# Logits of an attention unit: from three tiled visits on four PSUM banks to two visits on six

## The chip, the cores and the metric

The kernel runs on one core of a Trainium2 chip. The metric is the time of one execution on the device, in microseconds (us). All executions told of here are fast, with a granted TensorE clock of 0.997 to 1.000. Engines are called PE (TensorE), PEld (its weight loads), DVE (VectorE), ACT (ScalarE), POOL (GpSimd) and SP (which issues DMAs). "Start to start" is the time between the recorded starts of two matmuls in the trace; I use it rather than durations, because matmuls are pipelined (a full one is recorded 380 ns long, and the next starts after 216) and their recorded ends are modelled.

## The reference, cut to what matters

A layer norm of x (2048 tokens x 1024), then the sum of x, an attention branch and a token-mixing MLP. The attention has 32 heads of 32 channels and 4 segments of 512 tokens:

```python
for s in range(N):                                   # 4 segments
    logits = jnp.einsum('bhqd,bhkd->bhqk', qs, ks) * scale + mask   # causal, 512 x 512
    p = _softmax(logits, axis=-1)
    a_dot = jnp.einsum('bhqk,bhkd->bhqd', p, vs)
    pq = phi(qs)
    ...                                              # memory read: a_mem = pq M / (pq z)
    o = g * a_mem + (1.0 - g) * a_dot
    pk = phi(ks)
    M = M + jnp.einsum('bhld,bhle->bhde', pk, vs)    # memory update
    ...
return o @ wo
```

## The kernel before

Four heads of one segment are a *unit*; there are 32. For each unit PE computes logits (transposed: keys on the partitions), ACT takes Exp out of PSUM, POOL sets the masked triangle of the diagonal blocks to zero, and PE weighs the values with the result. Keys come in four blocks of 128. For key block kb only the queries from 128 kb on count, so a head needs 512, 384, 256 and 128 columns for blocks 0 to 3: 1280 float32 columns. The kernel divides PSUM, the memory that PE writes to, into eight banks of 512 such columns.

A head has 32 channels, so its logits matmul fills only 32 of the 128 rows of PE's array. The kernel puts the four heads of a unit on the four 32-row tiles, each writing to its own bank, and they stream side by side (four starts within 10 ns in the trace). I call one such stay in the tiled mode a *visit*. Between visits PE runs full-array matmuls that it has anyway, of the MLP and of the output projection (`main_emit(n)` emits n of them, each 512 columns).

```python
PT_OFF = [0, 512, 896, 1152]
...
    LOGIT_STEPS = [[0], [1], [2, 3]]

    def logits(self, u, step):
        ...
        with fw.group(reads=[self.R_kT[k], self.R_qT[k]], writes=self.R_bank[0:4]):
            col = 0
            for kb in kbs:
                n_q = SEG_L - P * kb
                for r in range(4):
                    fw.mm(self.ps[:, r, col:col + n_q], self.kT[k][32 * r:32 * r + 32, kb * P:(kb + 1) * P],
                          self.qT[k][32 * r:32 * r + 32, kb * P:SEG_L],
                          start=True, stop=True, tile_position=(32 * r, 0))
                col += n_q
        ...
        fw.op("act", lambda e: e.activation(self.pT[:, :, off:off + total], self.ps[:, 0:4, 0:total],
                                            ACT.Exp, scale=SCALE), ...)
        ...                                  # POOL: affine_select on each diagonal block
```

The loop over units (cut); `weigh` of query block qb uses bank 4 + qb % 2, the projections of the unit after next use banks 0, 1 and 2, the full matmuls accumulate in banks 6 and 7:

```python
            self.logits(u, 0)
            self.main_emit(n0)
            ...
            self.logits(u, 1)
            self.main_emit(n1)
            self.logits(u, 2)
            ...
            self.main_emit(n2)
            self.weigh(u, 0)
            self.weigh(u, 1)
            self.proj_q(un, 0)          # ACT evacuates; Exp of q from the second segment on
            self.weigh(u, 2)
            self.proj_v(m, u % 4, 2)
            self.weigh(u, 3)
            self.proj_k(un, 1)          # DVE evacuates, then ACT takes Exp ("etmp") of the same bank
            self.main_emit(n3)
...
            return (10, 8, 7, 7) if u < N_GRP else (10, 8, 8, 8)     # n0..n3; the last units differ
```

The softmax here doesn't subtract the row's maximum and nothing guards it: scores larger than these inputs give would overflow.

Of the kernel before, what the change touches and what calls it, by code (L numbers as in the profile page):

```python
# [6 lines left out]
ACT = mybir.ActivationFunctionType  # L7
# [9 lines left out]
SEG_L = 512  # L17
F_MLP = 3584
P = 128
# [3 lines left out]
SCALE = float(D_HEAD) ** -0.5  # L23
# [5 lines left out]
N_GRP = N_HEAD // 4  # L29
N_UNIT = N_SEG * N_GRP  # L30
VW = D_HEAD + 1
GW = 4 * VW
PT_OFF = [0, 512, 896, 1152]
PT_COLS = 1280


# [279 lines left out]
def _after(*groups):  # L316

    toks = {}
    for r in groups:
        for t in list(r.r.values()) + ([r.w] if r.w is not None else []):  # L320
            cur = toks.get(t.key)
            if cur is None or cur.val < t.val:
                toks[t.key] = t
    return toks
# [21 lines left out]
class _Kernel:  # L346
# [428 lines left out]
        self.fw.dma(self.pk[j][:], self.mtmp[1][:], reads=[self.R_mtmp[1]], writes=[self.R_pk[j]], transpose=True)  # L775


    LOGIT_STEPS = [[0], [1], [2, 3]]

    def logits(self, u, step):  # L780
        fw = self.fw
        k = u % 3
        kbs = self.LOGIT_STEPS[step]
        total = sum(SEG_L - P * kb for kb in kbs)
        with fw.group(reads=[self.R_kT[k], self.R_qT[k]], writes=self.R_bank[0:4]):
            col = 0
            for kb in kbs:
                n_q = SEG_L - P * kb
                for r in range(4):
                    fw.mm(self.ps[:, r, col:col + n_q], self.kT[k][32 * r:32 * r + 32, kb * P:(kb + 1) * P],  # L790
                          self.qT[k][32 * r:32 * r + 32, kb * P:SEG_L],
                          start=True, stop=True, tile_position=(32 * r, 0))
                col += n_q
        off = PT_OFF[kbs[0]]
        fw.op("act", lambda e: e.activation(self.pT[:, :, off:off + total], self.ps[:, 0:4, 0:total],  # L795
                                            ACT.Exp, scale=SCALE),
              reads=self.R_bank[0:4],
              writes=[self.R_pTu[kb] for kb in kbs] + [self.R_pTd[kb] for kb in kbs])
        for kb in kbs:
            d = self.pT[:, :, PT_OFF[kb]:PT_OFF[kb] + P]  # L800
            fw.op("pool", lambda e: e.affine_select(d, d, pattern=[[0, 4], [1, P]], compare_op=ALU.is_ge,  # L801
                                                    fill=0.0, base=0, channel_multiplier=-1),
                  reads=[self.R_pTu[kb]], writes=[self.R_pTd[kb]])

    def weigh(self, u, qb):
# [14 lines left out]
        with fw.group(reads=reads, writes=[self.R_bank[b]]):  # L820
            for r in range(4):
                for kb in range(qb + 1):
                    col = PT_OFF[kb] + (qb - kb) * P
                    fw.mm(self.ps[:, b, VW * r:VW * r + VW], self.pT[:, r, col:col + P], vA[:, kb, hl + r, :],
# [121 lines left out]
    def attention_and_out(self):  # L946
        fw = self.fw
        self.main_init()
        fw.dma(self.wo_sb[:], self.A_wo.rearrange("(jc p) j -> p jc j", p=P), writes=[self.R_wo])
        self.stg_ring.ensure(0)  # L950
        self.proj_q(0, 4)
        self.proj_k(0, 5)
        self.k_transpose(0)
        self.gates()
        for c in range(4):
            self.proj_v(0, c, c)
        self.proj_q(1, 4)
        self.proj_k(1, 5)
        self.main_emit(8)

        def last_of_seg(u):
            return u % N_GRP == N_GRP - 1

        for u in range(N_UNIT):
            s = u // N_GRP
            un, m = u + self.LEAD, u // 4 + 1
            n0, n1, n2, n3 = self.share(u)
            if u == N_GRP:
                wait = _after(*[self.R_xnT[c] for c in range(4)])
                self.oT[1] = self.xnT[0]  # L970
                self.R_oT[1] = [Res(f"oT1_{g}", wait) for g in range(N_GRP)]
            self.logits(u, 0)
            if u and last_of_seg(u - 1):
                self.o_transpose_dma(u - 1)
            self.main_emit(n0)
            if u and not last_of_seg(u - 1):
                self.combine(u - 1)
            self.logits(u, 1)
            self.main_emit(n1)
            self.logits(u, 2)  # L980
            if u + 1 < N_UNIT and (u + 1) // N_GRP < N_SEG - 1:
                self.k_transpose(u + 1)
            if u and not last_of_seg(u - 1):
                self.o_transpose_dma(u - 1)
            self.main_emit(n2)
            self.weigh(u, 0)
            self.weigh(u, 1)
            if un < N_UNIT:
                self.proj_q(un, 0)
            else:  # L990
                self.main_emit(8)
            self.weigh(u, 2)
            if m < 2 * N_SEG:
                self.proj_v(m, u % 4, 2)
            self.weigh(u, 3)
            if un < N_UNIT:
                self.proj_k(un, 1)
            if last_of_seg(u):
                self.combine(u)
            self.main_emit(n3)  # L1000
        assert self.main_k == len(self.main)
        self.tail()

    @staticmethod
    def share(u):

        if u < N_UNIT - 4:
            return (10, 8, 7, 7) if u < N_GRP else (10, 8, 8, 8)
        return (10, 9, 8, 10) if u < N_UNIT - 2 else (10, 9, 8, 4)

    def tail(self):
        fw = self.fw
# [59 lines left out]
```

## Time and profile before

| | before |
|---|---|
| time, median of the first 3 runs | 704.21 us (703.87 to 705.7) |
| span of the profiled execution | 702.2 us |
| one unit, first logits matmul to the next unit's | 14.65 us in the first segment, 15.19 us in most later ones |

From the page of the kernel before: the busy time of each engine with its share of the span, and the chain of work that ended last, by engine.

```profile
PE 688.9 (98%) x4724; PEld 322.7 (46%) x4814; DVE 258.5 (37%) x578; ACT 277.5 (40%) x301; POOL 100.8 (14%) x156
...
PE 95%; DMA 1%; issue 1%; DVE 1%; SPq 0%; ACT 0%; ACTq 0%
```

PE is the bound, and the chain is PE almost from end to end. The list of PE's waits in the kernel before (who waited for whom, us in total, times, longest) says that it hardly ever waits:

```profile
PE ps_all L194 <- DVE h L661: 1.9, 1, 1.9
PE ps_all L194 <- issue: 1.6, 10, 0.2
PE ps_all L194 <- DVE brow_51 L518: 1.3, 1, 1.3
PE ps_all L194 <- DVE stg_1573 L939: 0.7, 1, 0.7
PE ps_all L200 <- DVE o_s_1564 L877: 0.2, 1, 0.2
```

So a change pays only if it shortens what PE itself does between one matmul and the next. The timeline of PE in the kernel before, around the three visits of unit 13 (start and length in us, then the instructions; L194 is the line of the helper that issues every matmul; `32*128` is a 32-row tile, x4 are four matmuls, and the shape shown is that of the first):

```profile
409.81 0.38 PE L194 MATMUL ps_all<-wo_sb,oT_1569 128*128 128x512 bf16 x1
410.12 0.40 PE L194 MATMUL ps_all<-qT_1550,kT_1553 32*128 32x512 bf16 x4
410.44 0.39 PE L194 MATMUL ps_all<-wo_sb,oT_1569 128*128 128x512 bf16 x1
...
412.40 0.38 PE L194 MATMUL ps_all<-gT,w2h_895 128*128 128x512 bf16 x1
412.71 0.34 PE L194 MATMUL ps_all<-qT_1550,kT_1553 32*128 32x384 bf16 x4
412.98 0.39 PE L194 MATMUL ps_all<-gT,w2h_895 128*128 128x512 bf16 x1
...
414.50 0.38 PE L194 MATMUL ps_all<-gT,w2h_895 128*128 128x512 bf16 x1
414.81 0.34 PE L194 MATMUL ps_all<-qT_1550,kT_1553 32*128 32x256 bf16 x8
415.09 0.39 PE L194 MATMUL ps_all<-gT,w2h_895 128*128 128x512 bf16 x1
```

Read the starts, not the lengths. Full matmuls follow one another every 216 ns. In front of a visit it is 0.31 us from the last full matmul to the first logits matmul (312 ns is the median of all visits), 96 ns more than a full matmul needs. Behind the visit it is 0.32, 0.27 and 0.15 us from the last logits matmul to the next full one (medians 317, 264 and 147 ns, after 512, 384 and 128 columns). At 512 columns in 216 ns, 384 take about 162 and 128 about 54 (estimates), so 93 to 102 ns of each are not streaming. A visit therefore costs about 200 ns of PE time on top of its columns. It is the tiled mode, not the smallness of the matmuls: the weighing matmuls have 33 columns each, run on the full array, and start 25 ns apart, and the next projection's first matmul starts 26 ns after the last of them. The Trainium skill, "TensorEngine Tiling (Array Packing)", section Key Properties, states that changing the tiling mode drains the TensorE; these gaps are in line with that.

One more reading. In units 1 to 8 the first visit starts late. From the timeline of the kernel before, at unit 3:

```profile
259.23 0.81 PE L194 MATMUL ps_all<-gT,w2h_896 128*128 128x512 bf16 x3
259.35 0.60 ACT L758 ACTIVATE etmp_1566<-ps_all 128x512 bf16<-128x512 f32 x1 [2.55 <-DVE kT_1553 L755]
...
260.09 0.40 PE L194 MATMUL ps_all<-qT_1549,kT_1552 32*128 32x512 bf16 x4
```

The Exp of the next keys (`etmp`, out of bank 1) ends at 259.95, and the first logits matmul, which writes bank 1, starts 0.14 us after that. In these units it is 432 ns from the last full matmul to the first logits matmul in place of 312.

### The profile page before, as it was taken

Reading aid. Unit: us, or ns where it says so; the run is one execution under the profiler, and the core shown is the slowest. Engines: PE = TensorE matmul, PEld = TensorE weight load, DVE = VectorE, ACT = ScalarE, POOL = GpSimd, SP = SyncE. Lnnn points to the kernel's source line nnn. Section 1 sums busy time; section 2 is a strip of 40 time slices with the busy share of each in tenths; the row PEclk is TensorE's granted clock in tenths of the full one; section 3 lists DMA queues with packets and bytes.
Section 4 is the critical chain, followed back from the end, with each engine's and each line's share of the span. In section 5 each row is a group of like instructions: output and inputs, shape, how many; then the busy total and the mean of one; then the engine's idle time right before and its main releaser. Section 6 shows DMA issues by size and latency. Waiting matters only on the chain.

```text
span 702.2 us, 11155 instructions
## 1 busy us (share of the span) xinstructions
PE 688.9 (98%) x4724; PEld 322.7 (46%) x4814; DVE 258.5 (37%) x578; ACT 277.5 (40%) x301; POOL 100.8 (14%) x156
## 2 busy tenths in 40 slices
PE   8999999999999999999999999999999999999998
PEld 3444444444444444444444444444444444444443
DVE  7730000000012333343454454545546553434444
ACT  7522111111134445444544444444444444443440
POOL 3600000000001111211121211112211111211120
DMA  9497694226044537556264543526173444537003
GB/s 323 98 225 176 139 234 125 61 60 139 1 159 92 114 60 145 120 94 118 50 133 98 112 100 75 128 46 143 34 170 88 86 95 78 114 69 120 23 16 135
DMA packets 210393, 77.17 MB, mean 110 GB/s; under 512 B 172840, under 2 KB 202792, under 8 KB 210344
## 3 DMA queue, kind: packets, MB, share of 16 engines
q1 hardware_dynamic: 209928, 76.06, 47.8%
q8 instruction: 38, 0.62, 0.4%
q10 hardware_dynamic: 416, 0.39, 0.2%
q14 instruction: 11, 0.09, 0.0%
HBM read 59.79 MB, written 5.24 MB: 93 GB/s over the span
## 4 chain that ended last, share of the span: by engine, by line
PE 95%; DMA 1%; issue 1%; DVE 1%; SPq 0%; ACT 0%; ACTq 0%
PE ps_all L194 95%; DMA xin<-in_A_x_dram 1%; SPq L216 0%; DVE prod L873 0%; DVE stg_1573 L939 0%; DVE stg_1571 L939 0%; DVE kT_1552 L755 0%; DVE fin_7784 L1031 0%; DVE ost_1562 L835 0%; ACT etmp_1566 L758 0%; DVE h L661 0%; DVE o_s_1564 L877 0%; PE ps_all L200 0%; DVE srec L871 0%; DVE mtmp_1568 L726 0%
## 5 line engine op out<-in xcount | busy, mean ns | idle before, releaser
L795 ACT ACTIVATE pT<-ps_all 128x1536 bf16<-128x1536 f32 (+1 forms) x96 | 152.9, 1593 | 93.9 <-PE ps_all L194 93.9
L801 POOL TENSOR_SCALAR_AFFINE_SELECT pT<-pT 128x512 bf16<-128x512 bf16 x128 | 84.6, 673 | 564.6 <-ACT pT L795 564.6
L717 ACT ACTIVATE gT<-ps_all,b1c 128x512 bf16<-128x512 f32 x56 | 37.7, 690 | 139.1 <-PE ps_all L194 133.6
L755 DVE CAST kT_1552<-ps_all 128x512 bf16<-128x512 f32 x11 | 7.6, 691 | 170.4 <-PE ps_all L194 170.4
L194 PE MATMUL ps_all<-h,w1s_80 128*128 128x512 bf16 x251 | 55.6, 379 | 0.3
L194 PE MATMUL ps_all<-h,w1s_81 128*128 128x512 bf16 x251 | 55.6, 379 | 0.3
L194 PE MATMUL ps_all<-h,w1s_79 128*128 128x512 bf16 x250 | 55.4, 379 | 0.3
L194 PE MATMUL ps_all<-gT,w2h_895 128*128 128x512 bf16 x219 | 55.1, 380 | 0.4 <-issue 0.2
L194 PE MATMUL ps_all<-gT,w2h_893 128*128 128x512 bf16 x220 | 53.9, 380 | 1.0 <-DVE stg_1573 L939 0.7
L194 PE MATMUL ps_all<-gT,w2h_894 128*128 128x512 bf16 x215 | 53.8, 380 | 0.9 <-issue 0.6
L194 PE MATMUL ps_all<-gT,w2h_896 128*128 128x512 bf16 x217 | 53.9, 380 | 0.6 <-issue 0.3
L835 DVE CAST ost_1561<-ps_all 128x264 bf16<-128x264 f32 (+1 forms) x64 | 23.8, 394 | 64.4 <-PE ps_all L194 64.2
L194 PEld LDWEIGHTS ps_all<-h,w1s_80 128*128 128x128 bf16 x256 | 25.0, 98 | 30.2
L194 PEld LDWEIGHTS ps_all<-h,w1s_79 128*128 128x128 bf16 x256 | 25.0, 98 | 30.2
L194 PEld LDWEIGHTS ps_all<-h,w1s_81 128*128 128x128 bf16 x256 | 25.0, 98 | 30.2
L758 ACT ACTIVATE etmp_1566<-ps_all 128x512 bf16<-128x512 f32 x24 | 14.3, 597 | 58.8 <-DVE kT_1554 L755 20.7
L835 DVE CAST ost_1562<-ps_all 128x264 bf16<-128x264 f32 (+1 forms) x64 | 23.7, 394 | 37.2 <-PE ps_all L194 37.0
L194 PEld LDWEIGHTS ps_all<-gT,w2h_893 128*128 128x128 bf16 x224 | 20.4, 98 | 26.6 <-issue 4.6
L194 PEld LDWEIGHTS ps_all<-gT,w2h_896 128*128 128x128 bf16 x224 | 20.4, 98 | 25.3 <-issue 3.5
L194 PEld LDWEIGHTS ps_all<-gT,w2h_894 128*128 128x128 bf16 x224 | 20.1, 98 | 25.2 <-issue 4.0
L194 PEld LDWEIGHTS ps_all<-gT,w2h_895 128*128 128x128 bf16 x224 | 20.0, 98 | 25.2 <-issue 4.5
L194 PE MATMUL ps_all<-wo_sb,oT_1569 128*128 128x512 bf16 x124 | 30.4, 380 | 0.3 <-issue 0.2
(154 smaller groups left out, 838.6 us busy)
## 6 DMA issues: line engine op xcount, KB each, us to landing
w1s_81<-in_B_w_dram SPq DMA_DIRECT2D x4, 1024.0 KB, 5.7
w1s_79<-in_B_w_dram SPq DMA_DIRECT2D x4, 1024.0 KB, 5.8
w1s_80<-in_B_w_dram SPq DMA_DIRECT2D x4, 1024.0 KB, 5.7
wq_889<-in_A_wq_dram SPq DMA_DIRECT2D x16, 256.0 KB, 4.5
wq_890<-in_A_wq_dram SPq DMA_DIRECT2D x16, 256.0 KB, 3.5
wk_891<-in_A_wk_dram SPq DMA_DIRECT2D x16, 256.0 KB, 4.8
wk_892<-in_A_wk_dram SPq DMA_DIRECT2D x16, 256.0 KB, 3.8
w2h_893<-in_B_w_dram SPq DMA_DIRECT2D x8, 448.0 KB, 4.8
```

The costliest lines, as they stand in the source:

```text
L194: ins = self.nc.tensor.matmul(*args, **kwargs)
L717: fw.op("act", lambda e: e.activation(self.gT[:, fc, half * 512:(half + 1) * 512], self.bank(b), ACT.Gelu_apprx_tanh, bias=self.b1c[:, fc: ...
L755: fw.op("dve", lambda e: e.tensor_copy(self.kT[k][:], self.bank(b)), reads=[self.R_bank[b]], writes=[self.R_kT[k]])
L758: fw.op("act", lambda e: e.activation(self.etmp[1][:], self.bank(b), ACT.Exp), reads=[self.R_bank[b]], writes=[self.R_etmp[1]])
L795: fw.op("act", lambda e: e.activation(self.pT[:, :, off:off + total], self.ps[:, 0:4, 0:total], ACT.Exp, scale=SCALE), reads=self.R_bank[0:4],
L801: fw.op("pool", lambda e: e.affine_select(d, d, pattern=[[0, 4], [1, P]], compare_op=ALU.is_ge, fill=0.0, base=0, channel_multiplier=-1), ...
L835: fw.op("dve", lambda e: e.tensor_copy(dst, self.ps[:, b, 0:n * VW]), reads=[self.R_bank[b]], writes=[self.R_ost[o][qb]])
```

## The change

The intent: two visits a unit in place of three. Blocks 0 and 2 (512 + 256 columns a head) make the first visit. The 1024 columns of block 2 go to banks 4 and 5, two heads to a bank. Blocks 1 and 3 (384 + 128 = 512) make the second, on banks 0 to 3. Two row tiles may not write one bank at the same time (the Trainium skill, "TensorEngine Tiling (Array Packing)", section Restrictions and Gotchas), so in the first visit block 2 of heads 0 and 2 comes first (group 1), then block 0 of all heads (group 2), then block 2 of heads 1 and 3 (group 3), and PE waits before group 3 until its own semaphore tells that group 1 is done. Exp still has three instructions (block 0, block 2, blocks 1 and 3), and the number of full matmuls in a unit stays.

```diff
-PT_OFF = [0, 512, 896, 1152]
+PT_OFF = [0, 768, 512, 1152]
...
-    LOGIT_STEPS = [[0], [1], [2, 3]]
+    LOGIT_STEPS = [[[(0, 2), (2, 2)], [(1, 0), (3, 0), (0, 0), (2, 0)], [(1, 2), (3, 2)]],
+                   [[(0, 1), (1, 1), (2, 1), (3, 1), (0, 3), (1, 3), (2, 3), (3, 3)]]]
...
+        for group in self.LOGIT_STEPS[step]:
+            if len(toks) == 2:
+                fw.E["pe"].eng.wait_ge(toks[0].sem, toks[0].val)
+            banks = self.R_bank[4:6] if group[0][1] == 2 else self.R_bank[0:4]
+            with fw.group(reads=[self.R_kT[k], self.R_qT[k]], writes=banks) as grp:
+                for r, kb in group:
+                    n_q = SEG_L - P * kb
+                    b, col = (4 + r // 2, 256 * (r % 2)) if kb == 2 else (r, 384 if kb == 3 else 0)
+                    fw.mm(self.ps[:, b, col:col + n_q], ...)
+            toks.append(grp.tok)
+        heads = self.ps[:, 0:4, :]
+        if step == 0:
+            self.weights((0,), heads, self.R_bank[0:4])
+            self.weights((2,), self.ps[:, 4:6, :].rearrange("p b (h q) -> p (b h) q", q=256), self.R_bank[4:6])
+        else:
+            self.weights((1, 3), heads, self.R_bank[0:4])
...                                    # weights(): Exp and the masks, as before
-            self.main_emit(n1)
-            self.logits(u, 2)
...
-            return (10, 8, 7, 7) if u < N_GRP else (10, 8, 8, 8)
-        return (10, 9, 8, 10) if u < N_UNIT - 2 else (10, 9, 8, 4)
+            return (11, 14, 7) if u < N_GRP else (11, 15, 8)
+        return (11, 16, 10) if u < N_UNIT - 2 else (11, 16, 4)
```

More of the change, by code (lines that the diff above doesn't have):

```diff
@@ L782, in logits, with weights @@
         k = u % 3
-        kbs = self.LOGIT_STEPS[step]
-        total = sum(SEG_L - P * kb for kb in kbs)
-        with fw.group(reads=[self.R_kT[k], self.R_qT[k]], writes=self.R_bank[0:4]):
-            col = 0
-            for kb in kbs:
-                n_q = SEG_L - P * kb
-                for r in range(4):
-                    fw.mm(self.ps[:, r, col:col + n_q], self.kT[k][32 * r:32 * r + 32, kb * P:(kb + 1) * P],
+        toks = []
+        for group in self.LOGIT_STEPS[step]:
[6 more added lines that the diff above has]
+                    b, col = (4 + r // 2, 256 * (r % 2)) if kb == 2 else (r, 384 if kb == 3 else 0)
+                    fw.mm(self.ps[:, b, col:col + n_q], self.kT[k][32 * r:32 * r + 32, kb * P:(kb + 1) * P],
                           self.qT[k][32 * r:32 * r + 32, kb * P:SEG_L],
                           start=True, stop=True, tile_position=(32 * r, 0))
-                col += n_q
-        off = PT_OFF[kbs[0]]
-        fw.op("act", lambda e: e.activation(self.pT[:, :, off:off + total], self.ps[:, 0:4, 0:total],
-                                            ACT.Exp, scale=SCALE),
-              reads=self.R_bank[0:4],
-              writes=[self.R_pTu[kb] for kb in kbs] + [self.R_pTd[kb] for kb in kbs])
+            toks.append(grp.tok)
[5 more added lines that the diff above has]
+            self.weights((1, 3), heads, self.R_bank[0:4])
+    def weights(self, kbs, src, R_src):
+        fw = self.fw
+        off, total = PT_OFF[kbs[0]], sum(SEG_L - P * kb for kb in kbs)
+        fw.op("act", lambda e: e.activation(self.pT[:, :, off:off + total], src, ACT.Exp, scale=SCALE),
+              reads=R_src, writes=[self.R_pTu[kb] for kb in kbs] + [self.R_pTd[kb] for kb in kbs])
         for kb in kbs:
@@ L966, in attention_and_out @@
             un, m = u + self.LEAD, u // 4 + 1
-            n0, n1, n2, n3 = self.share(u)
+            n0, n1, n2 = self.share(u)
             if u == N_GRP:
@@ L984, in attention_and_out @@
                 self.o_transpose_dma(u - 1)
-            self.main_emit(n2)
+            self.main_emit(n1)
             self.weigh(u, 0)
@@ L999, in attention_and_out @@
                 self.combine(u)
-            self.main_emit(n3)
+            self.main_emit(n2)
         assert self.main_k == len(self.main)
```

## The prediction

> **What bounds the kernel.** TensorE. The profile's first part has PE busy 688.9 of 702.2 us (98%), ACT 40%, DVE 37%, POOL 14%; the chain that ended last is 95% PE; the list of waits gives PE under 6 us of waiting in the whole span. So only PE's own issue time counts; ACT and POOL count only if late.
>
> **Cost of a logits visit now.** Full-array matmuls of 512 columns start every 216 ns (timeline). Start-to-start times around each logits visit (four 32-row tiles side by side), 32 units: last full matmul to first logits matmul 312 ns (96 more than 216); last logits matmul to next full matmul 317 ns after 512 columns, 264 after 384, 147 after 128, each the streaming plus about 100. So a visit pays about 200 ns for entering and leaving the tiled mode. The Trainium skill ("TensorEngine Tiling (Array Packing)", section Key Properties) says that changing the tiling mode drains TensorE; the trace agrees, at about 200 ns a pair. Whole visits, less one 216: step 0 423 ns, step 1 369, step 2 372: 1164 ns a unit. In units 1 to 7 step 0 also waits 120 ns for the Exp of the next keys, 145 ns before its first matmul.
>
> **What the change does.** Matmuls, masks and full matmuls stay; Exp elements too (2048 + 1024 + 2048 in place of 2048 + 1536 + 1536; durations 1.88 and 1.45 us give about 1.02 for 1024, so the sum stays 4.78). It removes one visit a unit: 200 ns x 32 = 6.4 us, all on PE's critical path. Part is given back: in the new step 0 rows 1 and 3 may not write banks 4 and 5 until rows 0 and 2 are done, so the third group waits for PE's own semaphore (same page, Gotcha 1: row tiles may not use one bank at once; no trace here shows a collision). The first 256-column pair is recorded 278 ns long, and its semaphore moves about 28 ns after the recorded end; [...] the third group starts 340 to 400 ns after the first matmul, where the rows are free at about 220. The next full matmul follows 210 ns later.
>
> New step 0: 311 + about 370 + 210 - 216 = 675 (650 to 710). New step 1: 372 + 53 for the longer columns = 425. Together 1100 in place of 1164: 64 ns x 32 = 2.0 us. The 120 ns waits of units 1 to 7 hide behind the first group (banks 4, 5): 0.8 us more.
>
> **New lateness?** Exp of blocks 1 and 3 should end 5.4 us after the unit's first logits matmul, the mask of block 1 at 6.1 (6.4 where DVE slows POOL, seen as 0.93 in place of 0.63 us); the weighing that needs it starts at 6.5 (first segment) to 6.8. Slack 0.3 to 0.7 us: no stall.
>
> **Prediction:** 701.6 us, 8 in 10 between 699.6 and 704.0. Faster by over 2%: 0.01; within 2%: 0.98; slower: 0.01.
>
> **What would show it.** Right: two visits a unit; step 0 near 675 ns, step 1 near 425; PE waits still few; ACT busy unchanged; unit period 60 to 190 ns shorter (now 14.65 and 15.19 us). Wrong: third group at 220 ns (saving 5 us or more), or over 450 (none).
>
> **What would make it wrong.** Release from the own semaphore slower than taken, or row tiles of unlike lengths not streaming side by side; POOL's mask late, so that weighing stalls; a chip that differs by more than these 3 us.

## The result, and the profile after

| | before | changed |
|---|---|---|
| time, median of 4 runs each | 704.77 us (703.87 to 705.7) | 700.17 us (699.74 to 701.33) |
| ratio | | 0.9937, 95% interval 0.9918 to 0.9957 |
| span of the profiled execution | 702.2 us | 698.3 us |
| one unit, first segment / most later ones | 14.65 / 15.19 us | 14.43 / 15.09 us |

A ratio is the mean time of one kernel's fast runs over that of the other's in the same rounds, so it is not quite the ratio of the medians quoted. The kernel became 0.6% faster, which is clear of the noise. It is inside the predicted range and beyond its middle: 4.6 us by the medians and 3.9 by the spans, where the prediction's terms gave 2.8.

From the page of the changed kernel, the same two lines: PE still bounds it, and ACT's busy time is 1.3% less with the same elements: the Exp of block 2 starts 0.1 us before that of block 0 is recorded as ended, so the two overlap in the records.

```profile
PE 686.6 (98%) x4724; PEld 326.1 (47%) x4814; DVE 258.8 (37%) x578; ACT 273.9 (39%) x301; POOL 102.5 (15%) x156
...
PE 96%; DMA 1%; DVE 1%; issue 1%; SPq 1%; ACT 0%; ACTq 0%
```

PE's waits in the changed kernel (the first three of five): still few. The wait on its own semaphore is not among them, because matmuls of groups 1 and 2 are still recorded as running while it lasts.

```profile
PE ps_all L194 <- DVE h L661: 1.8, 1, 1.8
PE ps_all L194 <- DVE brow_51 L518: 1.3, 1, 1.3
PE ps_all L194 <- DVE stg_1573 L952: 0.5, 1, 0.5
```

The timeline of PE in the changed kernel around the two visits of unit 13:

```profile
407.66 0.38 PE L194 MATMUL ps_all<-wo_sb,oT_1569 128*128 128x512 bf16 x1
407.98 0.63 PE L194 MATMUL ps_all<-qT_1550,kT_1553 32*128 32x256 bf16 x8
408.54 0.39 PE L194 MATMUL ps_all<-wo_sb,oT_1569 128*128 128x512 bf16 x1
...
410.70 0.38 PE L194 MATMUL ps_all<-gT,w2h_895 128*128 128x512 bf16 x1
411.02 0.40 PE L194 MATMUL ps_all<-qT_1550,kT_1553 32*128 32x384 bf16 x8
411.35 0.39 PE L194 MATMUL ps_all<-gT,w2h_895 128*128 128x512 bf16 x1
```

And the weight loads of the first of these visits (PEld), which show the groups. Loads of groups 1 and 2 go out together; those of group 3 come 0.35 us after the first, released by PE itself:

```profile
407.97 0.11 PEld L194 LDWEIGHTS ps_all<-qT_1550,kT_1553 32*128 32x128 bf16 x6 [0.42 <-issue]
408.32 0.10 PEld L194 LDWEIGHTS ps_all<-qT_1550,kT_1553 32*128 32x128 bf16 x2 [0.23 <-PE ps_all L194]
408.53 0.11 PEld L194 LDWEIGHTS ps_all<-wo_sb,oT_1569 128*128 128x128 bf16 x2
```

The stretch from the first logits matmul of unit 0 to the start of the last weighing matmul holds all that the change touches. Busy time by engine in that stretch, the kernel before:

```profile
core 0: us, PE busy (x) PEld busy (x) DVE busy (x) ACT busy (x) POOL busy (x), PEclk, DMA share, GB/s
216.16:684.53 468.37, 462.48 (x3697) 220.25 (x3767) 213.56 (x469) 212.47 (x200) 84.62 (x128) 1.00 0.45 92
```

and the changed kernel:

```profile
core 0: us, PE busy (x) PEld busy (x) DVE busy (x) ACT busy (x) POOL busy (x), PEclk, DMA share, GB/s
216.33:680.64 464.31, 459.93 (x3698) 223.71 (x3767) 213.97 (x469) 208.94 (x200) 86.08 (x128) 1.00 0.45 93
```

The stretch is 468.4 before and 464.3 us after: 4.07 us shorter by the exact starts. It is my measure for all experiments, because it repeats: a second profile of the changed kernel has 464.28. What lies ahead of it does not. In the twelve traces, whose opening is the same code, the first logits matmul starts at 216.0 to 218.6 us. From the last weighing matmul to the end it is 17.66 to 17.68 us in all twelve, and the two traces of the changed kernel differ by 1.4 us both in span and in opening. So here the opening makes the spread. Executions of the kernel before over all rounds lie between 703.80 and 707.85 us; the slowest of them have no trace, so what made them slow is not shown.

Where the 4.07 us came from, by starts in the trace. The cost of a visit is from the last full matmul before it to the first full matmul behind it, less one 216; medians of 32 units:

| part | before | changed | difference |
|---|---|---|---|
| visits of a unit | 423 + 369 + 372 = 1164 ns | 657 + 426 = 1083 ns | 81 ns x 32 = 2.6 us |
| first full matmul behind a visit: 226 ns to the next in place of 216 | 3 x 10 ns | 2 x 10 ns | 10 ns x 32 = 0.3 us |
| first visit waits for the Exp of the next keys | 120 ns in 8 units | hidden | 1.0 us |
| one late evacuation, unit 11 (start to start) | 1068 ns | 831 ns | 0.2 us |
| a new wait in unit 8 (below) | none | 0.1 us | -0.1 us |
| sum | | | 4.0 us |

The new wait: in unit 8 of the changed kernel the first output projection (`wo_sb`) starts at 336.36 us, 0.14 us after the DMA transpose of its input has landed (336.23), and 332 ns after the matmul before it in place of 216. Unit 8 takes 15.21 us, against 15.19 before and 15.09 in the units after it.

### The profile page after: what moved, and what is told of

Same layout as the page of the kernel before. It is cut to its first block, busy times and chain, and to the rows that moved or that the text cites. A ratio compares the mean times of both kernels' runs of the same rounds, so it can differ in the third digit from the quotient of the medians.

```text
span 698.3 us, 11157 instructions
## 1 busy us (share of the span) xinstructions
PE 686.6 (98%) x4724; PEld 326.1 (47%) x4814; DVE 258.8 (37%) x578; ACT 273.9 (39%) x301; POOL 102.5 (15%) x156
## 4 chain that ended last, share of the span: by engine, by line
PE 96%; DMA 1%; DVE 1%; issue 1%; SPq 1%; ACT 0%; ACTq 0%
PE ps_all L194 95%; DMA xin<-in_A_x_dram 1%; SPq L216 1%; DVE prod L886 0%; DVE stg_1573 L952 0%; DVE stg_1571 L952 0%; DVE kT_1552 L755 0%; DVE fin_7820 L1042 0%; DVE ost_1562 L848 0%; ACT etmp_1566 L758 0%; DVE h L661 0%; DVE o_s_1564 L890 0%; PE ps_all L200 0%; DVE srec L884 0%; DVE mtmp_1568 L726 0%
## 5 line engine op out<-in xcount | busy, mean ns | idle before, releaser
L810 ACT ACTIVATE pT<-ps_all 128x2048 bf16<-128x2048 f32 (+1 forms) x96 | 149.4, 1591 | 58.9 <-PE ps_all L194 57.9
L814 POOL TENSOR_SCALAR_AFFINE_SELECT pT<-pT 128x512 bf16<-128x512 bf16 x128 | 86.1, 685 | 557.4 <-ACT pT L810 556.2
L194 PE MATMUL ps_all<-gT,w2h_895 128*128 128x512 bf16 x219 | 54.3, 380 | 0.4
L194 PE MATMUL ps_all<-gT,w2h_893 128*128 128x512 bf16 x221 | 53.7, 380 | 0.7 <-DVE stg_1573 L952 0.5
L194 PE MATMUL ps_all<-gT,w2h_894 128*128 128x512 bf16 x214 | 53.3, 380 | 0.6 <-issue 0.2
L194 PE MATMUL ps_all<-gT,w2h_896 128*128 128x512 bf16 x217 | 53.1, 380 | 0.5 <-issue 0.2
L194 PEld LDWEIGHTS ps_all<-gT,w2h_896 128*128 128x128 bf16 x224 | 21.0, 98 | 25.4 <-issue 1.5
L194 PEld LDWEIGHTS ps_all<-gT,w2h_894 128*128 128x128 bf16 x224 | 20.8, 98 | 25.8 <-issue 1.9
L194 PEld LDWEIGHTS ps_all<-gT,w2h_893 128*128 128x128 bf16 x224 | 20.7, 98 | 25.9 <-issue 2.2
L194 PEld LDWEIGHTS ps_all<-gT,w2h_895 128*128 128x128 bf16 x224 | 20.8, 98 | 24.9 <-issue 1.3
```

The source lines that it names most:

```text
L194: ins = self.nc.tensor.matmul(*args, **kwargs)
L814: fw.op("pool", lambda e: e.affine_select(d, d, pattern=[[0, 4], [1, P]], compare_op=ALU.is_ge, fill=0.0, base=0, channel_multiplier=-1), ...
```

## The experiments

Theory T1: what counts is the number of visits. A visit less saves about 210 ns a unit, and the wait for the own semaphore gives more than half of that back, on the critical path. Rivals: T2, the gain comes from the new banks and the new grouping of Exp and columns, not from the visits; T3, the wait is hidden behind other streaming and costs nothing.

The stretch is from the first logits matmul to the last weighing matmul, as above. Every ratio is to the kernel before in the same rounds. The record marks every run as correct, also the two that are wrong. So the check doesn't notice when weights of another head or key block are used: by the input scales of the reference the scaled logits have a spread of about 0.0025 (an estimate), and every Exp is close to 1. "Correct" therefore says little here about the logits.

| run | median us | ratio to before (95%) | stretch us | against the changed kernel's stretch |
|---|---|---|---|---|
| before | (see ratio) | | 468.38 | +4.07 |
| changed | 700.17 | 0.9937 (0.9918 to 0.9957) | 464.31 | |
| b_regroup | 704.04 | 0.9989 (0.9971 to 1.0007) | 468.39 | +4.08 |
| a_split | 706.99 | 1.0031 (1.0013 to 1.0049) | 471.14 | +6.83 |
| a_longwait | 708.31 | 1.0043 (1.0020 to 1.0065) | 471.06 | +6.75 |
| a_nowait (wrong) | 697.16 | 0.9898 (0.9877 to 0.9920) | 461.38 | -2.93 |
| a_late2 | 699.68 | 0.9928 (0.9910 to 0.9946) | 463.70 | -0.61 |
| b_n3 | 704.28 | 0.9993 (0.9975 to 1.0011) | 468.21 | +3.90 |
| a_nowait_n3 (wrong) | 696.91 | 0.9889 (0.9868 to 0.9909) | 460.34 | -3.97 |
| a_shift | 700.93 | 0.9935 (0.9917 to 0.9953) | 463.70 | -0.61 |
| after_again (changed kernel, again) | 700.72 | 0.9931 (0.9910 to 0.9953) | 464.28 | -0.03 |
| a_best | 699.19 | 0.9913 (0.9892 to 0.9934) | 462.77 | -1.54 |

### b_regroup: the grouping without the fewer visits

```diff
-PT_OFF = [0, 512, 896, 1152]
+PT_OFF = [0, 768, 512, 1152]
-    LOGIT_STEPS = [[0], [1], [2, 3]]
+    LOGIT_STEPS = [[0], [1, 3], [2]]
-            return (10, 8, 7, 7) if u < N_GRP else (10, 8, 8, 8)
+            return (10, 10, 5, 7) if u < N_GRP else (10, 10, 6, 8)
```

(The shares n0 to n3 of the last four units change likewise.)

> The kernel before with the key blocks regrouped as the change groups them (0, then 1 and 3, then 2; Exp of 2048, 2048 and 1024 columns) but in three visits on four banks; full matmuls split 10, 10, 6 so that Exp has time. Theory T1 (what counts is the number of visits to the tiled mode): visits of about 423, 426 and 310 ns, together 1159 against 1164 before, so the same time as before within 1 us, units of 14.65 and 15.19 us. Rival T2 (the gain comes from the new grouping of Exp and of the columns): most of the 4.4 us gain shows here, 700 to 701 us.

Measured: 704.04 us, ratio 0.9989 with 1 inside the interval; visits of 423, 425 and 316 ns, 1164 together; units of 14.65 and 15.19 us; a stretch of 468.39 us against 468.38. Regrouping blocks and Exp alone, on four banks in three visits, is worth nothing. T2 loses its first half.

### a_split: the changed kernel with a third visit again

```diff
-                   [[(0, 1), (1, 1), (2, 1), (3, 1), (0, 3), (1, 3), (2, 3), (3, 3)]]]
+                   [[(0, 1), (1, 1), (2, 1), (3, 1)], [(0, 3), (1, 3), (2, 3), (3, 3)]]]
...
         for group in self.LOGIT_STEPS[step]:
+            if step == 1 and toks:
+                self.main_emit(1)
...                                   # and one full matmul less behind the second step
```

> The changed kernel with its second visit cut in two: block 1, one full matmul, block 3, and one Exp after both as before; six banks, own wait and Exp grouping stay. T1: visits 657, 369 and about 252 ns, together 195 more than the 1083 of the changed kernel, and 10 ns more for the slow first full matmul after the extra visit: 205 ns x 32 = 6.6 us longer than the changed kernel, about 706.7 us, so slower than before by 2 us. T2 (banks and Exp grouping): stays at 700 us.

Measured: 706.99 us, a stretch 6.83 us longer than the changed kernel's (expected 6.6). The three visits cost 656, 370 and 273 ns. Timeline of PE in this run around block 1, the one full matmul and block 3:

```profile
413.54 0.38 PE L194 MATMUL ps_all<-gT,w2h 128*128 128x512 bf16 x1
413.85 0.34 PE L194 MATMUL ps_all<-qT,kT 32*128 32x384 bf16 x4
414.12 0.39 PE L194 MATMUL ps_all<-gT,w2h 128*128 128x512 bf16 x1
414.44 0.23 PE L194 MATMUL ps_all<-qT,kT 32*128 32x128 bf16 x4
414.61 0.39 PE L194 MATMUL ps_all<-gT,w2h 128*128 128x512 bf16 x1
```

The same columns with one more visit cost 1298 in place of 1083 ns a unit (medians): a visit by itself is about 215 ns of PE time. Six banks, the own wait and the Exp of the change are all still there, and the kernel is slower than the one before. T2 is out.

### a_longwait: the own wait made longer

```diff
-                fw.E["pe"].eng.wait_ge(toks[0].sem, toks[0].val)
+                fw.E["pe"].eng.wait_ge(toks[1].sem, toks[1].val)
```

> The changed kernel with the own wait made longer: the third group waits for the second group (512 columns) in place of the first. T1 with the wait on the critical path: the third group starts about 560 ns after the first logits matmul in place of 346, step 0 costs about 870 ns in place of 657, 215 ns x 32 = 6.9 us longer than the changed kernel, about 707 us. Rival T3 (the wait hides behind the other row tiles' streaming and the drain): less than 2 us longer.

Measured: 708.31 us; first visit 872 ns; stretch 6.75 us longer (expected 6.9). The weight loads of one first visit in this run; group 3 is loaded 0.56 us after the first load:

```profile
412.91 0.11 PEld L194 LDWEIGHTS ps_all<-qT,kT 32*128 32x128 bf16 x6 [0.42 <-issue]
413.47 0.09 PEld L194 LDWEIGHTS ps_all<-qT,kT 32*128 32x128 bf16 x2 [0.45 <-PE ps_all L194]
```

The wait's length goes into the time nearly one for one. T3 is out from this side. Most of the wait doesn't depend on the columns waited for: group 3 starts 343 ns after the last 256-column matmul of group 1 in the changed kernel, and here 440 ns after the last 512-column matmul of group 2. So 256 columns more add 97 ns, and about 245 ns of the 343 stay (estimate from these two starts).

### a_nowait: the own wait gone, with other buffers

Dropping the wait alone would let two row tiles write one bank unordered. So here the third group writes to banks 1 and 3, each head over its own block 0, and Exp of block 2 reads the half of banks 4 and 5 that is written. The result is wrong; the matmuls and Exp sizes are the same.

```diff
-            if len(toks) == 2:
-                fw.E["pe"].eng.wait_ge(toks[0].sem, toks[0].val)
-            banks = self.R_bank[4:6] if group[0][1] == 2 else self.R_bank[0:4]
+            banks = self.R_bank[4:6] if group[0] == (0, 2) else self.R_bank[0:4]
...
-                    b, col = (4 + r // 2, 256 * (r % 2)) if kb == 2 else (r, 384 if kb == 3 else 0)
+                    b, col = (4 + r // 2, 0) if kb == 2 and r % 2 == 0 else (r, 384 if kb == 3 else 0)
...
-            self.weights((2,), self.ps[:, 4:6, :].rearrange("p b (h q) -> p (b h) q", q=256), self.R_bank[4:6])
+            self.weights((2,), self.ps[:, 4:6, None, 0:256].to_broadcast([P, 2, 2, 256]), self.R_bank[4:6])
...                                   # and Exp's output is viewed in the same shape
```

> The changed kernel with the third group (heads 1 and 3 of block 2) written to banks 1 and 3, over their own block 0, so that no two row tiles share a bank and the own wait goes. The result is wrong on purpose. Same matmuls and Exp sizes. T1: third group starts at about 228 ns, step 0 costs about 540 ns in place of 657, 117 ns x 32 = 3.8 us shorter than the changed kernel, about 696.4 us. T3 (the wait is hidden, or row tiles of unlike lengths do not stream side by side): no shorter than 699.5 us.

Measured: 697.16 us; first visit 532 ns in place of 657; third group 234 ns after the first matmul in place of 346. All eight weight loads of the visit now go out together:

```profile
407.45 0.12 PEld L194 LDWEIGHTS ps_all<-qT,kT 32*128 32x128 bf16 x8 [0.42 <-issue]
407.89 0.11 PEld L194 LDWEIGHTS ps_all<-wo_sb,oT 128*128 128x128 bf16 x2 [0.32 <-issue]
```

So row tiles of 256 and 512 columns do stream side by side, and the own wait costs 125 ns a visit. That is 4.0 us over 32 units, nearly all that the change gains. The two visits together cost 958 ns without it, 206 less than the three before; with the 10 ns behind a visit that is the size of a_split's 215 again. But the stretch became only 2.93 us shorter, where I expected 3.8. Units 1 to 7 got hardly shorter (14.42 us against 14.43), nor did unit 8 (15.21 in both); unit 0 and nearly all units from 9 on did by 0.12.

### a_nowait_n3: why the first segment did not get shorter

```diff
-            return (11, 14, 7) if u < N_GRP else (11, 15, 8)
+            return (11, 13, 8) if u < N_GRP else (11, 15, 8)
```

(on a_nowait; wrong likewise)

> The kernel without the own wait (wrong on purpose) with the same move of one full matmul in the first segment. Without the wait units 0 to 7 did not get shorter than in the changed kernel (14.42 against 14.43 us), where units from 9 on did by 0.12. If the keys' Exp, up to 120 ns late for the second group there, is the reason: within the first visit about 237 ns in all units, units 1 to 7 about 14.31 us, 0.9 us shorter than the run without the wait, about 696.2 us. If not: unchanged at 14.42 us.

Measured: units 0 to 7 take 14.30 us, the first visit 532 ns in every unit, and the stretch is 460.34 us, 1.05 less than without the move (0.9 expected; unit 8 gives 0.12 more than its visit, because its wait for the transpose is gone too). In the changed kernel's trace group 2 starts 119 to 121 ns after the first matmul in units 1 to 8 and 6 to 7 ns in all others, while group 3 starts at 345 to 348 ns in all of them. So the late Exp of the keys, 120 ns in front of the first visit before, is hidden behind group 1 and the own wait after the change; taking the own wait away brings it out again. Two waits that run at the same time cost what the longer one costs.

### b_n3: the same wait taken out of the kernel before

```diff
-            return (10, 8, 7, 7) if u < N_GRP else (10, 8, 8, 8)
+            return (10, 8, 6, 8) if u < N_GRP else (10, 8, 8, 8)
```

> The kernel before with one full matmul of each unit of the first segment moved from behind the third visit to behind the key projection, so that the keys' Exp is done when the next unit's first visit comes. If the 120 ns in front of the first visit of units 1 to 8 are that wait: entry 312 ns in all units, those units 14.53 us in place of 14.65, 7 to 8 x 0.12 = 0.8 to 1.0 us shorter than before, about 703.3 us. If it is something else: unchanged.

A miss. The 312 ns in front of the first visit are there in all units, so the wait was the Exp of the keys; but units of the first segment take 14.62 to 14.63 us in place of 14.65, and the stretch is 0.17 us shorter, not 0.8. The timeline of this run at unit 3 shows where it went: Exp of the third visit on ACT, and the first matmuls of the query projection, which write bank 0:

```profile
267.14 1.45 ACT L795 ACTIVATE pT<-ps_all 128x1536 bf16<-128x1536 f32 x1 [0.66 <-PE ps_all L194]
...
268.73 1.46 PE L194 MATMUL ps_all<-xnT,wq 128*128 128x512 bf16 x6
```

Exp ends at 268.59, and the projection starts 0.14 us later: PE now waits there (127 ns from the last weighing matmul to the projection, where it is 26 ns without a wait). In the kernel before the same projection started 0.26 us after Exp's end and had no need to wait. So in the first segment of the kernel before two limits lay close behind each other. The change does away with the second as well: its last Exp out of banks 0 to 3 ends 5.25 us after block 0's first matmul in units 1 to 7, where the kernel before ends its third at 6.55, so bank 0 is free long before the projection.

### a_late2: another place for the third group

```diff
-    LOGIT_STEPS = [[[(0, 2), (2, 2)], [(1, 0), (3, 0), (0, 0), (2, 0)], [(1, 2), (3, 2)]],
-                   [[(0, 1), (1, 1), (2, 1), (3, 1), (0, 3), (1, 3), (2, 3), (3, 3)]]]
+    LOGIT_STEPS = [[[(0, 2), (2, 2)], [(1, 0), (3, 0), (0, 0), (2, 0)]],
+                   [[(1, 1), (3, 1), (0, 1), (2, 1), (1, 3), (3, 3), (0, 3), (2, 3)], [(1, 2), (3, 2)]]]
...                                   # the own wait, on group 1 of the first visit, now in the second; Exp of block 2
                                      # after that of 1 and 3; shares 10, 15 and 10, 16 for 11, 14 and 11, 15
```

> The changed kernel with heads 1 and 3 of block 2 moved from the first visit to the end of the second, Exp of block 2 after that of 1 and 3, shares 10 and 16 in place of 11 and 15; correct. The own wait is long met by then, but heads 1 and 3 stand idle for 256 columns in the first visit and heads 0 and 2 in the second. T1: first visit about 532 ns (as the run without the wait), second about 425 + 125 = 550, together 1082 against 1082 of the changed kernel: the same time within 1 us (699 to 701), but in the first segment the keys' Exp holds the first visit up again, up to 0.1 us a unit longer. A theory in which the wait is a loss that any other place for the third group saves: 3 us shorter, 697 us.

Measured: visits of 525 and 528 ns, 1053 together in place of 1083; the stretch 0.61 us shorter; 699.68 us, which the timing doesn't separate from the changed kernel. As T1 says, the loss is mostly moved: the first visit gets 132 ns shorter, the second 102 longer, because heads 0 and 2 stand idle at its end. My 1082 was 29 ns a unit too high: I had put the second visit at 550.

### a_shift: the one late evacuation

```diff
+        if 8 <= u < 12:
+            return (11, 18 if u == 11 else 14, 8)
```

> The changed kernel with one full matmul less in each of units 8, 9 and 10 and three more in unit 11 (behind the second visit), so that the end of an output half in unit 11 comes 0.65 us later, when VectorE has done the keys' work that held its evacuation up. Correct. The one stall of PE on an evacuation (about 0.5 us in unit 11) goes, the masks stay in time: 0.5 us shorter than the changed kernel in the trace (697.8 us span in place of 698.3), too little for the timing to tell.

Measured: the wait for the evacuation is gone from the list of waits, and the stretch is 0.61 us shorter (expected 0.5). The time, 700.93 us, doesn't show it, as expected: this run's profile has its first logits matmul at 217.79 us, 1.5 us later than in the first profile of the changed kernel.

### after_again and a_best: the correct parts together

a_best is a_late2 with the shares of a_shift and one full matmul moved as in b_n3:

```diff
+        if 8 <= u < 12:
+            return (10, 19 if u == 11 else 15, 8)
...
-            return (10, 15, 7) if u < N_GRP else (10, 16, 8)
+            return (10, 14, 8) if u < N_GRP else (10, 16, 8)
```

> The changed kernel as it is, to be timed on the same chip and in the same rounds as the combination next to it, and to see how much of the spread between executions lies ahead of the attention part. Expected as at first: 700.2 us, 464.3 us from the first logits matmul to the last weighing matmul.

> Correct. Third group in the second visit (0.6 us shorter than the changed kernel from the first logits matmul to the last weighing matmul), the output half of unit 11 moved (0.6 us), and one full matmul moved behind the key projection in the first segment, which did nothing for the kernel before because the query projection then waited for the third Exp, but gave 1.05 us where the own wait was gone. If these add: 2.0 to 2.3 us shorter than the changed kernel, 462.2 us in that stretch, about 698.1 us. If the first segment gives the move back as in the kernel before: 1.2 us, 463.1 us in that stretch.

Measured in the same rounds: changed kernel 700.72 us (ratio 0.9931), a_best 699.19 us (0.9913), stretches of 464.28 and 462.77 us. It is the shortest correct kernel here by the trace, 1.5 us less than the changed one, of which a_late2 and a_shift explain 1.2; the intervals of the timing overlap. The expectation allowed 462.2 us or 463.1, and the result lies between. The move in the first segment gave only 0.02 us a unit (14.40 against 14.42 in a_late2): in a_late2 the keys' Exp is already hidden behind block 2 of heads 0 and 2. It also ended unit 8's wait for the transpose: that unit takes 14.84 us where a_late2's 15.21 less one full matmul (0.216) is 14.99.

### What is left open

The own wait costs 4 us, and I found no correct layout of eight banks that drops it without leaving row tiles idle elsewhere. Heads 1 and 3 start block 2 only after their own 512 columns, when group 1's 256 columns should long have streamed, so the order of each row tile might be enough without a semaphore. I did not run that: it takes the wait away and leaves what it guards, and the check would not see wrong logits. Also open is whether the roughly 100 ns on each side of a visit are the drain itself or weight loads that can't be hidden across it; in every trace the weight load on either side of the change starts about 4 ns before its matmul (at most 32), where between full matmuls of the kernel before it starts 214 ns ahead, and a load is recorded 90 to 98 ns long, the size of the gap. So the loads are a full rival of the drain, and no run here tells the two apart. It is also not shown why the opening of the kernel, ahead of the first logits matmul, differs by up to 2.6 us between executions.

## Why the prediction was right, and where its sizes were off

- **What bounds the kernel**: right. Only PE's own time counted; Exp's grouping alone changed nothing (b_regroup).
- **One visit less saves 200 ns a unit**: right in its mechanism and nearly in size. a_split measured 215 ns for a visit alone. The prediction missed that the first full matmul behind a visit takes 226 ns to the next one in place of 216, which is 10 ns a unit, 0.3 us.
- **The own wait gives part back**: right; a_nowait and a_longwait show it to be on the critical path. The size was off: "the third group starts 340 to 400 ns after the first matmul", with 370 put into the sum. It was 346, the low end: 66 ns lie between the recorded end of group 1 and the start of group 3, where 370 leaves about 90. The semaphore moved 18 to 19 ns after the recorded end, where the kernel before had shown 28, and group 3 started 47 ns after that. So the first visit cost 657 ns and not 675, which is 0.6 us over 32 units. The 210 ns from there to the next full matmul were right (208 to 211).
- **The second visit**: 425 predicted, 426 measured.
- **"The 120 ns waits of units 1 to 7 hide behind the first group"**: right, and there were eight such units, 1 to 8: 1.0 us and not 0.8. a_nowait_n3 shows that they are hidden, not gone. b_n3 shows that the kernel before could not have had this microsecond by moving one matmul.
- **No new lateness**: right. Exp of blocks 1 and 3 ends 5.36 us after block 0's first matmul in most units (5.4 predicted), the mask of block 1 at 6.0 to 6.1, at most 6.4 apart from unit 11 (6.1 and 6.4 predicted), and the weighing that needs it starts at 6.5 in the first segment and 6.8 in most later units. A lateness that the prediction didn't look for did come: the 0.1 us of unit 8.
- **The time**: the mis-sized terms are 0.6 + 0.3 + 0.1 us (the last is the eighth waiting unit), the shorter stall in unit 11 adds 0.2, and unit 8 takes 0.1 back: 1.1 of the 1.3 us between the 2.8 that the terms gave and the 4.07 of the stretch. Most of the rest is rounding: unrounded, the terms gave 2.9. The 4.6 us of the medians hold the spread of the opening besides.

## What to carry to other kernels

Where PE is the bound and matmuls that fill few rows of the array run in row tiles between full-array ones, count the changes of tiling mode as well as the columns: measure start to start across one visit in the trace, and merge visits where spare PSUM banks allow it. Then look at what the merging costs: sharing a bank between row tiles was paid for here with a wait for a group of matmuls to end, and that cost 125 of the 215 ns that a visit less had saved. And a wait that disappears may only be hidden behind another one, so before spending work on it, take the other away in an experiment.

## What the Trainium skill lacked or had wrong

- "TensorEngine Tiling (Array Packing)", section Key Properties, says that a change of the tiling mode drains the TensorE and gives no cost. Here the gaps at the changes were 96 ns going in, 93 to 102 coming out, and 10 more until full matmuls were back at 216 ns apart; 215 ns in all for one more visit with the same columns (a_split).
- The same page, section Restrictions and Gotchas (Gotcha 1), says that row tiles may not use one PSUM bank at once and that software must see to it, not what that costs. ("TensorE: Matmul & The Clock Gate", Part 3, has a formula for the tail that semaphore increments add to packed matmuls, which no run here varied.) Seeing to it with PE's own semaphore put 346 ns between the start of the 256-column matmuls and the next pair in that bank, against 234 where nothing was shared. Nor does it say whether the order of the matmuls within each row tile would be enough; no run here tried.
- "TensorE: Matmul & The Clock Gate", Part 3, gives about 4 ns from tile to tile for packed matmuls; these traces agree (four starts within 10 ns). Its model has one length for all tiles; in a_nowait pairs of 256 and of 512 columns streamed side by side, and the whole visit of 768 columns a head cost 532 ns.
